# Causal attention and a routed feed-forward layer in one kernel: one set of transposes in place of two, and a table one slot later

## The chip, the cores and the metric

The kernel runs on one NeuronCore of a Trainium2 chip. The core has five engines that work side by side, each with its own queue in program order: TensorE (PE) multiplies matrices and transposes, VectorE (DVE) and ScalarE (ACT) work on elements and may read the accumulators in PSUM, GpSimd (POOL) works on elements in SBUF alone, and SyncE (SP) issues DMA transfers. An engine waits for another one by semaphores. The metric is the device time of one execution in microseconds (us), less is better.

## What is computed

The reference is causal attention for 8 batches, 12 heads, 448 tokens and 64 elements per head, followed by a layer of 8 experts in which each token goes to one expert and each expert keeps only its 80 tokens of largest weight:

```python
scores = np.where(mask, -1e9, scale * np.matmul(q, k.transpose(0, 1, 3, 2)))
attn = softmax(scores)
x = (attn @ v).transpose(0, 2, 1, 3).reshape(N, D)        # N = 3584 tokens, D = 768
logits = x @ w_gate                                        # 8 experts
expert_idx = np.argmax(logits, axis=1)
gate_w = probs[np.arange(N), expert_idx]
...
for e in range(E):
    tok_idx = np.where(expert_idx == e)[0]
    if len(tok_idx) > capacity:                            # capacity = 80
        gw = gate_w[tok_idx]
        tok_idx = tok_idx[np.argpartition(-gw, capacity)[:capacity]]
    out[tok_idx] = gate_w[tok_idx, None] * (np.maximum(x[tok_idx] @ w1[e], 0) @ w2[e])
```

The kernel must find, while attention still runs, the 80 best tokens of each expert. It does so batch by batch, with a table of the best 80 so far.

## The kernel before

**Attention in slots.** The 48 pairs of heads (8 batches of 6) run one after another, each in 8 slots. Slots 0 to 6 of a pair hold its seven blocks of scores (PE, L423 to L436, tile `sp`), each followed by a softmax on DVE (L445) and ACT (L448). In slots 0, 2, 4 and 6 PE also transposes a bank of the previous pair's weights (`tp`, L465, copied out by ACT, L477), and in slot 7 it multiplies weights and values of the pair before that (`xp`, L495). `sp` has three PSUM banks, `tp` two.

**Steps in slots.** Everything else is put into this run by a hand-written order. The dictionary `STEPS` gives for each step the slot, counted from the end of the batch that it belongs to, so 48 slots on is the same place for the next batch. The seventh batch has its own dictionary, `EARLY`, and the last one a written list, `TAIL`, which runs after attention. Within a slot the scores come first (in slot 6 of a pair, and so in slots 30 and 38 below, a turn of `tp` comes first, then the steps, then the scores), and steps of the earlier batch come before those of the later one. Each step's instructions stand in their engines' queues in just this order.

**The steps that matter here**, for one batch:

- `columns` (L698 to L708) writes on POOL the one-hot of each token's expert three times (`oh3`, L702) and the token's block and place (L703, L705) into `mv`.
- `parts` (L710 to L716) splits the token's gate weight on POOL into three bf16 parts in `mv`; its last instruction is L716.
- `r0t`, `r0c`: PE transposes `oh3` (four 128x128 bf16 transposes into a bank `selt`, L731) and DVE copies the 24 rows into `ex[:, 0]` (L734). `r1t`, `r1c` do the same for the three parts of the weight, into `ex[:, 1]`.
- `rl`, `lt` (L757 to L769): products of `ex[:, 0]` with the table's row, and DVE counts per token how many in the table are larger. `cp`, `ro` turn this into new places for the table.
- `c3w`, `c3l` to `c0w`, `c0l` (L742 to L750): all tokens of a batch against each other, four blocks, PE (tile `rn`) and then DVE. `gt` (L799) counts them.
- `rr`, `rr_more` (L846): DVE writes, in two halves, which token goes to which place. `tn` (L853): PE's products with these, which make the new table. `tab` copies it out (DVE, L873), `rp` transposes it (PE, L877), and `row` copies the row that the next batch's `rl` uses (DVE, L881). In the slots of the next batch, `tn`, `tab`, `rp` and `row` stand at 29, 30, 32 and 33.
- `rt` (L592) transposes finished attention rows, and DVE (L611) scales and stores them.

All PSUM tiles of these steps share two banks, `ps_m`. A tile gets the bank that was freed first in program order, that is, whose last reader comes first in it.

```python
nc.tensor.transpose(selt[:, t * P:(t + 1) * P], src, identb)               # L731
(nc.scalar.copy if last else nc.vector.tensor_copy)(bt.ex[0:3 * E, i], got[0][0:3 * E])   # L734
nc.tensor.matmul(rl[:, t, 0:sn], bt.ex[:, 0, t * P:(t + 1) * P], row[:, 0:sn], start=True, stop=True)   # L761
```

The splits of q and k for the next heads (L384 to L395, on DVE and POOL) run through the same queues; L387 is DVE's cast of k.

After attention the experts' two layers run (from L1127 on); the change does not touch them.

Of the kernel before, what the change touches and what calls it, by code (L numbers as in the profile page):

```python
# [10 lines left out]
BF16 = mybir.dt.bfloat16  # L11
# [6 lines left out]
P = 128  # L18
# [11 lines left out]
ROWGAP = 1  # L30
ROWS0 = [2, 3, 7, 13]
ROWS1 = [59, 62, 64, 65]
STEPS = {'gp': 18, 'gs': 18, 'lp': 21, 'lg': 22, 'logit': 23, 'shifted': 25, 'chosen': 26, 'sums': 27, 'one_hot': 28, 'weight': 28, 'weighted': 31, 'columns': 30, 'parts': 33, 'r0t': 32, 'r0c': 33, 'r1t': 34, 'r1c': 35, 'rl': 36, 'lt': 36, 'c3w': 38, 'c3l': 39, 'cp': 40, 'ro': 41, 'c2w': 41, 'c2l': 43, 'c1w': 43, 'c1l': 44, 'c0w': 46, 'c0l': 46, 'gt': 47, 'earlier': 51, 'own': 47, 'rank': 51, 'places': 63, 'places_more': 66, 'rr': 73, 'tn': 77, 'tab': 78, 'rp': 80, 'row': 81, 'rr_more': 75}
EARLY = {'gp': 18, 'gs': 18, 'lp': 21, 'lg': 21, 'logit': 22, 'shifted': 24, 'chosen': 26, 'sums': 27, 'one_hot': 28, 'weight': 29, 'weighted': 31, 'columns': 30, 'parts': 32, 'r0t': 33, 'r0c': 33, 'r1t': 34, 'r1c': 34, 'rl': 35, 'lt': 35, 'c3w': 36, 'c3l': 37, 'cp': 38, 'ro': 39, 'c2w': 39, 'c2l': 40, 'c1w': 40, 'c1l': 41, 'c0w': 41, 'c0l': 42, 'places': 43, 'places_more': 43, 'gt': 44, 'earlier': 44, 'own': 44, 'rank': 46, 'rr': 46, 'tn': 48, 'tab': 50, 'rp': 51, 'row': 52, 'rr_more': 46}
ROWS_EARLY = [22, 26, 29, 43]
THIRD = [0, 0, 2, 2, 4, 6, 8]
THIRD_NEXT = [0, 0, 6, 2, 6, 4, 8]
# [15 lines left out]
def attention_then_moe(  # L53
# [12 lines left out]
    nc = tc.nc  # L66
    B, _, NP, S = qT.shape
    N, D = out.shape
    E = wg.shape[2]
# [3 lines left out]
    NT = (S + P - 1) // P  # L73
# [24 lines left out]
    def bank(shape, dtype, name):  # L98
        return (ps_x or ps_m).tile(shape, dtype, name=name, tag="x" if ps_x else "misc")
# [20 lines left out]
    NV = 5  # L120
# [11 lines left out]
    for r in range(2):  # L132
        t = akeep.tile([P, OFF_L + NT * P], F32, name=f"prob{r}")
# [7 lines left out]
    for r in range(2):  # L141
        t = akeep.tile([P, NT, PH * P], F32, name=f"vt{r}")
# [61 lines left out]
    def piece_parts():  # L204

        got = []
        k = PIECES[len(wload)][3]
        got.append(piece())
        half = PW // k // 2

        def part(j, x):
            t, src = got[0]
            nc.sync.dma_start(t[:, j, x * half:(x + 1) * half], src[:, j, x * half:(x + 1) * half])
        return [lambda j=j, x=x: part(j, x) for j in range(k) for x in range(2)]


    mv = one_hots = mv_flat = oh_flat = expert_cols = tables = table_rows = None
    identb = before = dec = number = number_after = pnum = tbase = wgd = slots_e = slots_t = None
# [3 lines left out]
    lg = keep.tile([P, NT, H * E], F32, name="lg")  # L222
# [28 lines left out]
    def late_constants():  # L251


        def padded(shape, name):
            t = spool.tile(shape, BF16, name=name, tag=name, bufs=1)
            nc.gpsimd.memset(t, 0.0)
            return t

        def orders():
            nonlocal identb, before  # L260
            identb = const.tile([P, P], BF16, name="identb")
            nc.gpsimd.tensor_copy(identb, ident)

            before = const.tile([P, NT * P], BF16, name="before")
            nc.gpsimd.memset(before, 1.0)
            own = before[:, (NT - 1) * P:NT * P]
            nc.gpsimd.affine_select(own, own, [[-1, P]], ALU.is_gt, 0.0, base=0, channel_multiplier=1)

        def gate_weights():
            nonlocal wgd  # L270

            wgd = const.tile([P, NP, 4 * E], F32, name="wgd")
            nc.gpsimd.memset(wgd, 0.0)
            for i in range(2):
                for j in range(2):
                    nc.gpsimd.tensor_copy(wgd[j * DH:(j + 1) * DH, i:NP:2, 2 * i + j:4 * E:4],
                                          wg_sb[j * DH:(j + 1) * DH, i:NP:2, :])

        def slots():
            nonlocal mv_flat, mv, slots_e, slots_t  # L280
            many = max(1, NSL)
            slots_e = const.tile([SL, many, E, SL], COUNT, name="slots_e")
            slots_t = const.tile([P, many, NT, SL], COUNT, name="slots_t")
            for t, k in ((slots_e, E), (slots_t, NT)):
                nc.gpsimd.iota(t, [[SL, many], [0, k], [1, SL]], base=0, channel_multiplier=0,
                               allow_small_or_imprecise_dtypes=True)
            mv_flat = padded([P, (NT - 1) * NV * E + 2 * E + P], "mv")
            mv = mv_flat[:, 0:NT * NV * E].rearrange("k (t v e) -> k t v e", v=NV, e=E)

        def operands():  # L290
            nonlocal oh_flat, one_hots, expert_cols, tables, table_rows
            oh_flat = padded([P, (NT - 1) * 3 * E + P], "oh3")
            one_hots = oh_flat[:, 0:NT * 3 * E].rearrange("k (t v e) -> k t v e", v=3, e=E)
            expert_cols = padded([P, 2, NT * P], "ex")
            tables = [[padded([SL, 2 * E + P], f"tab{s}_{i}") for i in range(2)] for s in range(NSL)]
            table_rows = [[padded([P, SL], f"row{s}_{i}") for i in range(2)] for s in range(NSL)]

        return [orders, gate_weights, slots, operands]
# [392 lines left out]
    def select_groups(bt):  # L691

        b = bt.b
        last = b == B - 1
# [2 lines left out]

        def columns():  # L698
            oh = bt.oh
            m, oh3 = bt.m, bt.oh3 = mv, one_hots  # L700
            bc = [P, NT, E]
            eng.tensor_copy(oh3, oh.unsqueeze(2).to_broadcast([P, NT, 3, E]))  # L702
            nc.gpsimd.tensor_tensor(out=m[:, :, 0, :], in0=oh, in1=tbase[:, b, :].unsqueeze(2).to_broadcast(bc),  # L703
                                    op=ALU.mult)
            nc.gpsimd.tensor_tensor(out=m[:, :, 1, :], in0=oh, in1=pnum.unsqueeze(2).to_broadcast(bc), op=ALU.mult)  # L705
            bt.parts = sm("parts", [P, NT])
            bt.less = [sm(f"less{t}", [P, (t + 1) * P], BF16) for t in range(NT)]
            bt.ex = expert_cols  # L708
# [14 lines left out]
        def expert_rows(i):  # L723
            got = []

            def turn():
                selt = bank([P, NT * P], BF16, "selt")
                got.append(selt)
                for t in range(NT):
                    src = mv_flat[:, (t * NV + 2) * E:][:, 0:P] if i else oh_flat[:, t * 3 * E:][:, 0:P]  # L730
                    nc.tensor.transpose(selt[:, t * P:(t + 1) * P], src, identb)  # L731

            def copy():
                (nc.scalar.copy if last else nc.vector.tensor_copy)(bt.ex[0:3 * E, i], got[0][0:3 * E])  # L734
            return [turn, copy]


        def compare(t):
            w = (t + 1) * P
            got = []  # L740

            def weights():  # L742
                rn = bank([P, NT * P], F32, "rn")
                got.append(rn)
                nc.tensor.matmul(rn[:, 0:w], bt.ex[:, 0, t * P:w], bt.ex[:, 1, 0:w], start=True, stop=True)

            def less():
                nc.vector.scalar_tensor_tensor(
                    out=bt.less[t], in0=got[0][:, 0:w], scalar=bt.gw[:, t:t + 1],
                    in1=before[:, NT * P - w:NT * P], op0=ALU.is_lt, op1=ALU.mult, accum_out=bt.parts[:, t:t + 1])  # L750
            return [weights, less]
# [90 lines left out]
        def move(s):  # L842
# [43 lines left out]
            if not last and NSL == 1:  # L886
# [3 lines left out]

        run = lambda fs: lambda: [f() for f in fs]
        bt.lower, bt.moves = [], []
        r0, r1 = expert_rows(0), expert_rows(1)
        cmp = [compare(t) for t in reversed(range(NT))]
        tabs = [table_chunk(s) for s in range(NSL)] if b else []
        moves = [f for s in range(NSL) for f in move(s)]
        steps = {"columns": columns, "parts": parts, "r0t": r0[0], "r0c": r0[1], "r1t": r1[0], "r1c": r1[1],
                 "places": places, "places_more": places_more, "earlier": earlier, "own": own, "rank": rank}
        steps.update({"hold": hold, **{f"gt{t}": lambda t=t: later_part(t) for t in range(NT)}} if last else {"gt": later})
        for t in range(NT):  # L900
# [38 lines left out]
    for b in range(B):  # L939
        bt = Batch()  # L940
# [17 lines left out]
    def batch_plan(bt):  # L958
# [12 lines left out]
        if CAP:  # L971
            steps.update(select_groups(bt))
        for name, at in (EARLY if early else STEPS).items():
            if name in steps:
# [7 lines left out]
    with tc.manual_schedule():  # L982
# [25 lines left out]
        deferred, parts = [], []  # L1008
        for i, pr in enumerate(pairs):
            bt = pr.bt  # L1010
# [20 lines left out]
            for k in range(SLOTS):  # L1031
                behind = []
                if k < SLOTS - 1:
                    work, after = scores[k]
                    turn, copy, x = turns[TSLOT.index(k)] if turns and k in TSLOT else (None, None, "a")
# [20 lines left out]
                if i > 4 and k % 4 == 3:  # L1056
                    if not parts and len(wload) < WBUF:
                        parts = piece_parts()
# [14 lines left out]
        bt = batches[-1]  # L1073
        turns = transpose_groups(pairs[n - 1])
        before_last, last_one = values_group(pairs[n - 2]), values_group(pairs[n - 1])
        steps = dict(zip(("guard", "invert", "last_rows"), norms(bt, slice(0, NP))))
# [3 lines left out]
        if CAP:  # L1080
            steps.update(select_groups(bt))
# [27 lines left out]
        for i, x in enumerate(ROW_ENGINES):  # L1109
            g, t = divmod(i, NT)  # L1110
# [331 lines left out]
```

## Time and profile before

| | us |
|---|---|
| median of 3 runs | 466.85 (466.36 to 467.3) |
| the profiled execution | 466.07 |
| its span, first to last instruction | 464.2 |
| one batch in the repeating part, 184.30 to 224.75 | 40.45 |
| busy in this batch: PE, DVE, ACT, POOL | 39.99, 37.63, 35.38, 34.73 |

The profile is of one execution. A line of its timeline gives start, duration, engine, line of the kernel, operation, and output and inputs with their shapes; "x4" is four instructions merged, and brackets give the engine's idle time just before and what ended it. PE's matmuls (PE) and the loads of their stationary operand (PEld) have rows of their own. Durations of neighbours overlap a little, since an engine begins one instruction while the last drains.

### The profile page before, as it was taken

To read this page: it belongs to the slowest core of one execution; us is meant where nothing else is said; L and a number is where in the kernel's file an instruction comes from. 1 tells how busy PE (TensorE), PEld (TensorE's weight loads), DVE (VectorE), ACT (ScalarE), POOL (GpSimd) and SP (SyncE) were. 2 spreads that over 40 slices of the span, in tenths; PEclk is the share of its full clock that TensorE was granted. 3 is DMA by queue.
4 is the path that set the end of the run, shared out by engine and by line. 5 is a ranking of instruction groups with operands and counts; after the bars stand their busy time and mean duration, and the time that the engine had idled before them with its cause. 6 is when DMAs were issued, how large, how long until landed. Compare 5 with 4: busy or idle time off the path is not lost.

```text
span 464.2 us, 14187 instructions
## 1 busy us (share of the span) xinstructions
PE 441.8 (95%) x4981; PEld 346.8 (75%) x4981; DVE 413.1 (89%) x1285; ACT 392.4 (85%) x1077; POOL 310.3 (67%) x382
## 2 busy tenths in 40 slices
PE   4899999999999999999999999999989999999994
PEld 2566667866777786677777767777648999999994
DVE  6888899988998999899899989989579999999892
ACT  6898989878988997898889789888586989988792
POOL 7999999988987987898798789860145133410011
PEclk9999999999999999999999999999999999999999
DMA  7758899989769578966957997539937999999941
GB/s 221 185 153 238 249 262 299 280 248 306 202 207 305 161 232 259 265 182 213 297 165 225 264 260 200 178 129 373 413 130 254 399 390 395 394 422 423 424 163 44
DMA packets 42998, 120.84 MB, mean 260 GB/s; under 512 B 6146, under 2 KB 23810, under 8 KB 39472
## 3 DMA queue, kind: packets, MB, share of 16 engines
q1 hardware_dynamic: 41712, 116.21, 76.9%
q0 software_dynamic: 1056, 3.51, 2.4%
q8 instruction: 39, 0.64, 0.6%
q14 instruction: 31, 0.25, 0.2%
q10 hardware_dynamic: 160, 0.23, 0.2%
HBM read 96.36 MB, written 23.99 MB: 259 GB/s over the span
## 4 chain that ended last, share of the span: by engine, by line
PE 83%; DVE 6%; DMA 3%; ACT 3%; issue 2%; SPq 1%; POOLq 0%; DVEq 0%
PE xp L495 16%; PE tp L465 15%; PE sp L423 6%; PE sp L424 5%; PE rt L592 4%; PE op L1245 4%; PE op L1237 4%; PE hp L1237 3%; PE gp L545 3%; PE hp L1252 3%; PE hp L1251 3%; PE hp L1249 3%; PE sp L433 3%; DMA qk<-k_t 3%; DVE ns L445 2%
## 5 line engine op out<-in xcount | busy, mean ns | idle before, releaser
L448 ACT ACTIVATE prob<-ns,nb 128x128 f32<-128x128 f32 (+3 forms) x336 | 177.0, 529 | 22.6 <-DVE nb L445 20.1
L445 DVE CUSTOM_DVE_ANT_0 ns<-sp,mask 128x384 f32<-128x384 f32 (+2 forms) x288 | 116.0, 413 | 18.7 <-PE sp L424 14.7
L465 PE MATMUL tp<-ident,prob 128*128 128x128 f32 x768 | 118.1, 276 | 0.9 <-ACT prob L448 0.9
L477 ACT COPY PT<-tp 128x512 f32<-128x512 f32 x182 | 104.0, 572 | 17.5 <-PE sp L423 8.4
L395 POOL TENSOR_TENSOR qk<-qk,qk 128x448 f16<-128x448 f32 x92 | 97.3, 1080 | 13.1 <-DVE qk L387 7.4
L465 PEld LDWEIGHTS tp<-ident,prob 128*128 128x128 f32 x768 | 89.6, 142 | 11.4 <-ACT prob L448 1.9
L1165 DVE SCALAR_TENSOR_TENSOR wl<-wraw,wh 128x768 f16<-128x768 f32 (+1 forms) x91 | 92.0, 1067 | 2.5 <-ACT wh L1180 2.3
L495 PE MATMUL xp<-PT,vt 128*64 128x448 f32 (+3 forms) x768 | 91.2, 380 | 0.0
L495 PEld LDWEIGHTS xp<-PT,vt 128*64 128x64 f32 x768 | 53.8, 137 | 42.7 <-issue 22.6
L423 PE MATMUL sp<-qk 128*128 128x384 f16 (+2 forms) x288 | 75.8, 279 | 8.0 <-DVE qk L349 5.1
L1180 ACT ACTIVATE wh<-wraw 128x768 f16<-128x768 f32 (+1 forms) x91 | 78.9, 931 | 4.2 <-PE hp L1252 1.8
L424 PE MATMUL sp<-qk 128*128 128x384 f16 (+2 forms) x288 | 78.1, 277 | 1.6 <-DVE qk L349 0.8
L448 ACT ACTIVATION_READ_ACCUMULATOR prob<-ns,nb 128x1 f32 x336 | 63.9, 190 | 0.0
L1338 POOL DMA_INDIRECT out<-yo,idx x8 | 14.6, 1828 | 69.0 <-ACT yo L1335 65.1
L390 POOL TENSOR_TENSOR qk<-qk,qk 64x448 f16<-64x448 f32 x46 | 54.2, 1179 | 3.4
L391 POOL TENSOR_TENSOR qk<-qk,qk 64x448 f16<-64x448 f32 x46 | 51.0, 1108 | 3.2
L387 DVE CAST qk<-qk 128x896 f16<-128x896 f32 x46 | 41.2, 897 | 1.1 <-DMA qk<-k_t 1.1
L423 PEld LDWEIGHTS <-qk 128*128 128x128 f16 x288 | 28.5, 99 | 17.1 <-issue 8.6
L384 POOL CAST qk<-qk 64x896 f16<-64x896 f32 x40 | 37.4, 936 | 4.3 <-PE sp L436 3.1
L1249 PEld LDWEIGHTS <-wh 128*128 128x128 f16 x362 | 36.5, 101 | 0.0
L1251 PEld LDWEIGHTS <-wh 128*128 128x128 f16 x362 | 36.2, 100 | 0.0
L1252 PEld LDWEIGHTS <-wl 128*128 128x128 f16 x362 | 36.2, 100 | 0.0
(192 smaller groups left out, 926.8 us busy)
## 6 DMA issues: line engine op xcount, KB each, us to landing
wraw<-w SPq DMA_DIRECT2D x27, 1536.0 KB, 20.4
qk<-k_t SPq DMA_DIRECT2D x92, 224.0 KB, 5.9
out<-mask_l SPq DMA_DIRECT2D x56, 192.0 KB, 4.4
qk<-q_t SPq DMA_DIRECT2D x23, 448.0 KB, 4.4
vt<-v_t SPq DMA_DIRECT2D x24, 384.0 KB, 5.9
xs<-xr SPq DMA_DIRECT2D x42, 192.0 KB, 3.9
wraw<-w SPq DMA_DIRECT2D x24, 256.0 KB, 6.1
vt<-v_t SPq DMA_DIRECT2D x24, 64.0 KB, 5.5
```

The costliest lines, as they stand in the source:

```text
L390: nc.gpsimd.tensor_tensor(out=qa[hi, i], in0=qf[lo, i], in1=qa[lo, i], op=ALU.subtract)
L391: nc.gpsimd.tensor_tensor(out=qb[lo, i], in0=qf[hi, i], in1=qb[hi, i], op=ALU.subtract)
L395: nc.gpsimd.tensor_tensor(out=k_lo[j][:, i], in0=kf[j][:, i], in1=k_hi[j][:, i], op=ALU.subtract)
L423: nc.tensor.matmul(sp[:, 0:w], qx[:, p, t * P:w], kx[:, p, 0:w], start=True, stop=False)
L424: nc.tensor.matmul(sp[:, 0:w], qx[:, p, t * P:w], lx[:, p, 0:w], start=False, stop=True)
L445: pr.masked = nc.vector.tensor_tensor_reduce(out=ns[:, 0:w], in0=sp[:, 0:w], in1=m, scale=-1.0 / 8.0, scalar=HUGE, op0=ALU.add, op1=ALU.mi ...
L448: nc.scalar.activation(pr.P[:, off:off + w], ns[:, 0:w], AF.Exp, bias=nb, scale=-1.0, accum_out=total)
L465: nc.tensor.transpose(pr.tp[:, i], pr.P[:, off:off + P], ident)
L477: copy(dst, src)
L495: state["pe"] = nc.tensor.matmul(xp[rows, 0:w], st["vt"][:, c, p * P + j * DH:p * P + (j + 1) * DH], pr.PT[:, j, n0:n0 + w], start=(c == 0 ...
L1165: return nc.vector.scalar_tensor_tensor(out=l, in0=src, scalar=SW, in1=h, op0=ALU.mult, op1=ALU.subtract)
L1180: nc.scalar.activation(h, src, AF.Copy, scale=SW)
```

## The change

For the first seven batches `mv` now has 128 columns per block of tokens, in 16 groups of 8: groups 2 to 6 hold what `mv` held, groups 8 to 10 the one-hots, and the others stay zero. So four transposes of whole blocks bring both sets of rows at once: the one-hots to partitions 64 to 87 and the weight's parts to partitions 32 to 55 of one bank. DVE still makes two copies out of it, at slots 33 and 35 (seventh batch: 33 and 34). The step is called `r1t` and stands where `r0t` stood (slot 32, seventh batch 33), and `parts` moves ahead of it, from 33 to 31. `tn`, `tab`, `rp` and `row` each come one slot later (78, 79, 81, 82 of their own batch; 30, 31, 33, 34 of the next). In the seventh batch `c0w` and `c0l` move from 41 and 42 to 42 and 43. The last batch keeps its two sets.

```diff
-STEPS = {... 'parts': 33, 'r0t': 32, 'r0c': 33, 'r1t': 34, 'r1c': 35, ... 'tn': 77, 'tab': 78, 'rp': 80, 'row': 81, 'rr_more': 75}
-EARLY = {... 'parts': 32, 'r0t': 33, 'r0c': 33, 'r1t': 34, 'r1c': 34, ... 'c0w': 41, 'c0l': 42, ...}
+STEPS = {... 'parts': 31, 'r1t': 32, 'r0c': 33, 'rl': 36, 'lt': 36, 'r1c': 35, ... 'tn': 78, 'tab': 79, 'rp': 81, 'row': 82, 'rr_more': 75}
+EARLY = {... 'parts': 32, 'r1t': 33, 'r0c': 33, 'r1c': 34, ... 'c0w': 42, 'c0l': 43, ...}
...
-            mv_flat = padded([P, (NT - 1) * NV * E + 2 * E + P], "mv")
-            mv = mv_flat[:, 0:NT * NV * E].rearrange("k (t v e) -> k t v e", v=NV, e=E)
+            mv_flat = padded([P, NT * P + 4 * E], "mv")
+            mv = mv_flat[:, 0:NT * P].rearrange("k (t v e) -> k t v e", t=NT, e=E)
...
-            m, oh3 = bt.m, bt.oh3 = mv, one_hots
+            m = bt.m = mv[:, :, 2:2 + NV, :]
+            oh3 = bt.oh3 = one_hots if last else mv[:, :, 8:11, :]
...
-                    src = mv_flat[:, (t * NV + 2) * E:][:, 0:P] if i else oh_flat[:, t * 3 * E:][:, 0:P]
+                    src = mv_flat[:, t * P + 4 * E:][:, 0:P] if i else oh_flat[:, t * 3 * E:][:, 0:P]
...
-                (nc.scalar.copy if last else nc.vector.tensor_copy)(bt.ex[0:3 * E, i], got[0][0:3 * E])
+                nc.scalar.copy(bt.ex[0:3 * E, i], got[0][0:3 * E])
             return [turn, copy]
+
+        def both_rows():
+            got = []
+
+            def turn():
+                selt = bank([P, NT * P], BF16, "selt")
+                got.append(selt)
+                for t in range(NT):
+                    nc.tensor.transpose(selt[:, t * P:(t + 1) * P], mv_flat[:, t * P:(t + 1) * P], identb)
+
+            def copy(i):
+                r = 4 * E if i else 8 * E
+                nc.vector.tensor_copy(bt.ex[0:3 * E, i], got[0][r:r + 3 * E])
+            return [turn, lambda: copy(0), lambda: copy(1)]
...
-        r0, r1 = expert_rows(0), expert_rows(1)
+        rows = [f for i in range(2) for f in expert_rows(i)] if last else both_rows()
...
-        steps = {"columns": columns, "parts": parts, "r0t": r0[0], "r0c": r0[1], "r1t": r1[0], "r1c": r1[1],
+        steps = {"columns": columns, "parts": parts, **dict(zip(("r0t", "r0c", "r1t", "r1c") if last else ("r1t", "r0c", "r1c"), rows)),
```

More of the change, by code (lines that the diff above doesn't have):

```diff
@@ L32 @@
 ROWS1 = [59, 62, 64, 65]
-STEPS = {'gp': 18, 'gs': 18, 'lp': 21, 'lg': 22, 'logit': 23, 'shifted': 25, 'chosen': 26, 'sums': 27, 'one_hot': 28, 'weight': 28, 'weighted': 31, 'columns': 30, 'parts': 33, 'r0t': 32, 'r0c': 33, 'r1t': 34, 'r1c': 35, 'rl': 36, 'lt': 36, 'c3w': 38, 'c3l': 39, 'cp': 40, 'ro': 41, 'c2w': 41, 'c2l': 43, 'c1w': 43, 'c1l': 44, 'c0w': 46, 'c0l': 46, 'gt': 47, 'earlier': 51, 'own': 47, 'rank': 51, 'places': 63, 'places_more': 66, 'rr': 73, 'tn': 77, 'tab': 78, 'rp': 80, 'row': 81, 'rr_more': 75}
-EARLY = {'gp': 18, 'gs': 18, 'lp': 21, 'lg': 21, 'logit': 22, 'shifted': 24, 'chosen': 26, 'sums': 27, 'one_hot': 28, 'weight': 29, 'weighted': 31, 'columns': 30, 'parts': 32, 'r0t': 33, 'r0c': 33, 'r1t': 34, 'r1c': 34, 'rl': 35, 'lt': 35, 'c3w': 36, 'c3l': 37, 'cp': 38, 'ro': 39, 'c2w': 39, 'c2l': 40, 'c1w': 40, 'c1l': 41, 'c0w': 41, 'c0l': 42, 'places': 43, 'places_more': 43, 'gt': 44, 'earlier': 44, 'own': 44, 'rank': 46, 'rr': 46, 'tn': 48, 'tab': 50, 'rp': 51, 'row': 52, 'rr_more': 46}
+STEPS = {'gp': 18, 'gs': 18, 'lp': 21, 'lg': 22, 'logit': 23, 'shifted': 25, 'chosen': 26, 'sums': 27, 'one_hot': 28, 'weight': 28, 'weighted': 31, 'columns': 30, 'parts': 31, 'r1t': 32, 'r0c': 33, 'rl': 36, 'lt': 36, 'r1c': 35, 'c3w': 38, 'c3l': 39, 'cp': 40, 'ro': 41, 'c2w': 41, 'c2l': 43, 'c1w': 43, 'c1l': 44, 'c0w': 46, 'c0l': 46, 'gt': 47, 'earlier': 51, 'own': 47, 'rank': 51, 'places': 63, 'places_more': 66, 'rr': 73, 'tn': 78, 'tab': 79, 'rp': 81, 'row': 82, 'rr_more': 75}
+EARLY = {'gp': 18, 'gs': 18, 'lp': 21, 'lg': 21, 'logit': 22, 'shifted': 24, 'chosen': 26, 'sums': 27, 'one_hot': 28, 'weight': 29, 'weighted': 31, 'columns': 30, 'parts': 32, 'r1t': 33, 'r0c': 33, 'r1c': 34, 'rl': 35, 'lt': 35, 'c3w': 36, 'c3l': 37, 'cp': 38, 'ro': 39, 'c2w': 39, 'c2l': 40, 'c1w': 40, 'c1l': 41, 'c0w': 42, 'c0l': 43, 'places': 43, 'places_more': 43, 'gt': 44, 'earlier': 44, 'own': 44, 'rank': 46, 'rr': 46, 'tn': 48, 'tab': 50, 'rp': 51, 'row': 52, 'rr_more': 46}
 ROWS_EARLY = [22, 26, 29, 43]
```

## The prediction

> **What bounds the kernel now.** I read the page first: busy shares, then the chain that ended last, then the groups by line with shapes kept apart.
>
> ```profile
> PE 441.8 (95%) x4981; PEld 346.8 (75%) x4981; DVE 413.1 (89%) x1285; ACT 392.4 (85%) x1077; POOL 310.3 (67%) x382
> PE 83%; DVE 6%; DMA 3%; ACT 3%; issue 2%; SPq 1%; POOLq 0%; DVEq 0%
> ```
>
> TensorE (PE) carries 83% of the chain, but VectorE (DVE) is busy 89% of the time, so little room separates them. What counts is which of the two ends last in each of the few stretches that the change touches. The transposes and copies in question are these groups:
>
> ```profile
> L731 PE MATMUL selt<-identb,oh 128*128 128x128 bf16 x32 | 3.1, 219 | 1.1 <-DVE oh L702 1.1
> L731 PE MATMUL selt<-identb,mv 128*128 128x128 bf16 x32 | 3.1, 217 | 0.2
> L734 DVE COPY ex<-selt 24x512 bf16<-24x512 bf16 x14 | 5.7, 405 | 0.0
> ```
>
> Both sets of transposes exist for all eight batches; seven lose one. The 14 DVE copies all stay: **DVE gets no work taken off.**
>
> Batches 2 to 6 (of 1 to 8) repeat one pattern. I take the fourth, from 183.7 us on, and first its timeline on every engine around the two sets (columns: start, duration, what ran, and in brackets the idle time before it). I number slots from the batch's end, as the schedule does.
>
> ```profile
> 187.02 0.32 DVE L849 TENSOR_TENSOR rr<-rank,slots_t 128x160 bf16<-128x160 f16 x1
> 187.38 0.25 PE L862 MATMUL tn<-mv,rr 128*80 128x40 bf16 x2 [0.32 <-DVE rr L849]
> 188.52 0.24 POOL L703 TENSOR_TENSOR mv<-goh,tbase 128x32 bf16<-128x32 f32 x1
> 190.04 0.25 POOL L716 TENSOR_TENSOR mv<-grest,mv 128x32 bf16<-128x32 f32 x1
> 190.71 0.29 DVE L445 CUSTOM_DVE_ANT_0 ns<-sp,mask 128x128 f32<-128x128 f32 x1 [1.18 <-PE sp L424]
> 190.74 0.10 PEld L877 LDWEIGHTS <-tab 80*128 80x128 bf16 x1
> 191.53 0.29 DVE L445 CUSTOM_DVE_ANT_0 ns<-sp,mask 128x128 f32<-128x128 f32 x1
> 191.74 0.18 DVE L881 COPY row<-rp 24x80 bf16<-24x80 bf16 x1
> 191.85 0.40 DVE L734 COPY ex<-selt 24x512 bf16<-24x512 bf16 x1
> 192.04 0.24 PEld L731 LDWEIGHTS <-mv 128*128 128x128 bf16 x4 [0.24 <-issue]
> 192.18 0.60 DVE L387 CAST qk<-qk 128x896 f16<-128x896 f32 x1
> 192.24 0.10 PEld L423 LDWEIGHTS <-qk 128*128 128x128 f16 x1
> 192.72 0.41 DVE L445 CUSTOM_DVE_ANT_0 ns<-sp,mask 128x256 f32<-128x256 f32 x1
> 193.06 0.41 DVE L445 CUSTOM_DVE_ANT_0 ns<-sp,mask 128x256 f32<-128x256 f32 x1
> 193.16 0.28 PEld L761 LDWEIGHTS <-ex 128*128 128x128 bf16 x4
> 193.40 0.41 DVE L734 COPY ex<-selt 24x512 bf16<-24x512 bf16 x1
> ```
>
> The reader is to see three things. PE waits 0.32 for the second half of `rr` inside the table's products (`tn`). At 190.71 DVE has been idle for 1.18 and waits for PE, so whatever PE saves before that point moves DVE forward too. From there DVE runs without a gap through both copies, while PE's `rl` weights (193.16) need two things that DVE writes: `row` and the first copy.
>
> **Part by part: one slot later for `tn`, `tab`, `rp`, `row`.** `tn` goes from slot 29 to slot 30, where it stands behind four transposes of attention weights (0.42 of PE, the row of 199.83 below). Then PE reaches the second half of `rr` after its end at 187.34, and the 0.32 goes. What is late next: nothing before 190.71, where DVE's 1.18 of idle time says that all its earlier work is done. Gain there: 0.33 (bound above: 0.42, if the transposes fill the wait and its restart whole). POOL's `columns` must not overwrite `mv` before `tn` has read it; before, `tn` ended at 187.63, now 0.1 to 0.3 later, and `mv` is written from 188.52 on: 0.6 of cover.
>
> In the second batch the wait is longer:
>
> ```profile
> 106.13 0.31 DVE L849 TENSOR_TENSOR rr<-rank,slots_t 128x160 bf16<-128x160 f16 x1
> 106.50 0.25 PE L862 MATMUL tn<-mv,rr 128*80 128x40 bf16 x2 [0.64 <-DVE rr L849]
> ```
>
> `rr` ends at 106.44 whatever PE does, so only the 0.42 of the transposes put in front is won.
>
> **One set instead of two.** The second set costs PE 0.24 of gap (192.04) and 0.20 until the next load (192.24), 0.44 per batch. The set that stays now needs `parts`, that is POOL's L716. In the steady batch that ends at 190.29 and PE, 0.33 earlier, gets there at about 190.4: no wait worth counting.
>
> But `rl` behind it gets nothing of this 0.44. `row` used to be DVE's next piece after the comparison of slot 33 (191.74). Now it stands behind the first copy (0.33 start to start), the cast (0.54) and the softmax of slot 34 (0.34): 1.21 later, so it ends at 193.13 less 0.33. PE, 0.33 + 0.44 earlier, would load `rl`'s weights at 192.4 and now waits until 192.85 or more. `rl` takes the bank of `rp`, which program order frees before that of the set, so the second copy doesn't hold it.
>
> **The copies' partitions.** Before, both copies read partitions 0 to 23. Now they read 64 to 87 and 32 to 55. No row shows DVE reading PSUM anywhere but from partition 0. The nearest rows are an early pair of casts (L384) on the lower and the upper half of the partitions:
>
> ```profile
> 23.10 0.61 DVE L384 CAST qk<-qk 64x896 f16<-64x896 f32 x1
> 23.64 0.61 DVE L445 CUSTOM_DVE_ANT_0 ns<-sp,mask_l 128x448 f32<-128x448 f32 x1
> 24.18 0.07 DVE L445 DVE_READ_ACCUMULATOR2_ANT nb<- 128x1 f32 x1
> 24.28 0.81 DVE L384 CAST qk<-qk 64x896 f16<-64x896 f32 x1
> 25.13 0.29 DVE L445 CUSTOM_DVE_ANT_0 ns<-sp,mask 128x128 f32<-128x128 f32 x1
> ```
>
> The lower cast's successor starts 0.07 before the cast ends (23.71 against 23.64). The upper cast starts 0.03 after its predecessor's end, and its successor 0.04 after its own: 0.11 lost on each side, 0.22 per visit to other partitions. Bounds for a copy: nothing (it writes partition 0, and only its read has moved) and 0.22; below nothing is excluded, since the copy's work is the same. I take 0.22, the row's value, so 0.44 of DVE per batch, half of it ahead of `row`.
>
> [...]
>
> With 0.22 ahead of `row`, `rl` loads at 193.07 instead of 193.16, and PE leaves it about 0.1 ahead of before. DVE, however, is 0.44 − 0.33 = 0.11 late after the second copy, and there the path changes engine:
>
> ```profile
> 196.22 0.61 ACT L448 ACTIVATE prob<-ns,nb 128x384 f32<-128x384 f32 x1 [0.66 <-DVE nb L445]
> 199.21 0.57 ACT L477 COPY PT<-tp 128x512 f32<-128x512 f32 x1
> 199.83 0.42 PEld L465 LDWEIGHTS tp<-ident,prob 128*128 128x128 f32 x4 [0.29 <-ACT PT L477]
> ```
>
> ScalarE (ACT) waits 0.66 for DVE's softmax of slot 37, then works without a gap up to the copy ending at 199.78, and PE already waits 0.29 for that copy. So this wait ends last: what DVE is late, PE is late at 199.83. A steady batch ends 0.11 later than before (bounds: 0.42 earlier without the holds, 0.12 later). The second batch: 0.44 − 0.42, nothing.
>
> **The first batch** has no table, and POOL is behind:
>
> ```profile
> 69.66 0.32 PEld L731 LDWEIGHTS <-oh 128*128 128x128 bf16 x4
> 70.40 0.25 POOL L716 TENSOR_TENSOR mv<-grest,mv 128x32 bf16<-128x32 f32 x1
> 70.41 0.29 DVE L445 CUSTOM_DVE_ANT_0 ns<-sp,mask 128x128 f32<-128x128 f32 x1 [0.32 <-PE sp L424]
> 70.96 1.04 DVE L387 CAST qk<-qk 128x896 f16<-128x896 f32 x1
> 72.40 0.32 PE L423 MATMUL sp<-qk 128*128 128x384 f16 x1 [0.27 <-DVE nb L445]
> ```
>
> The one set must wait for POOL's end at 70.65 where the first set started at 69.66. The loads start 1.04 later and the next scores about 0.9, DVE waits for them (it already does, 0.32), and PE's scores at 72.40 wait for DVE (0.27), so the missing second set gives nothing back. With 0.22 of holds and a cast that may run up to 0.4 shorter than 1.04: 0.7 to 1.1 lost, I take 0.95.
>
> **The seventh batch.** Its wait is another one:
>
> ```profile
> 309.25 0.31 PEld L592 LDWEIGHTS rt<-ident,xu 128*128 128x128 f32 x3 [0.38 <-PE tn L862]
> 313.78 0.18 DVE L881 COPY row<-rp 24x80 bf16<-24x80 bf16 x1
> 314.44 0.28 PEld L761 LDWEIGHTS <-ex 128*128 128x128 bf16 x4
> 320.90 0.10 PEld L423 LDWEIGHTS <-qk 128*128 128x128 f16 x1 [1.03 <-issue]
> ```
>
> With `tn` behind them the `rt` transposes needn't wait; `tn` waits for that bank instead, 0.15 won. `row` moves behind the copy and one softmax (0.33 + 0.34 + 0.22), so `rl` loads 0.3 later than 314.44. The last comparison's product one slot later shortens the 1.03 before 320.90, but the count behind it (`gt`) needs a DVE comparison whose time doesn't move. I take +0.26 (bounds −0.15 and +0.4). The last batch's steps and copies stay as they are.
>
> **Sum:** 0.95 + 0 + 4 × 0.11 + 0.26 = 1.65 us later. The profiled execution took 466.07 (span 464.2 and 1.9 around it), so 467.7 on its base; the median of the three runs lies 0.78 above, so **468.5**.
>
> **The rivals.**
> - **A, the forecast:** 468.5, own range 467.3 to 469.4. Chance 0.54.
> - **B, reads of upper PSUM partitions hold nothing** (not slower). For it: those copies write partition 0, and every held row here also writes elsewhere. Then DVE is 0.33 early at slot 37, ACT and the transposes of 199.83 too: 0.75 − 0.42 − 4 × 0.36 − 0.15 = −1.3, 465.5. It decides from 0.33 of holds per batch downwards. Chance 0.28.
> - **C, `row` isn't late either,** and PE keeps both gains: −0.77 in each steady batch, −0.9, −0.5, and 0.75 in the first: 463.1. Against it: DVE has no gap between 190.71 and `row`. Chance 0.09.
> - **D, `rl` waits for the second copy,** should the set's bank be the one it gets: ready at 193.81 + 0.44 − 0.33, PE some 0.5 late in each of five batches, with the first and seventh 470.8. Against it: program order. Chance 0.09.
>
> That the change doesn't remove the transposes is excluded: seven batches call one helper with one set.
>
> **The numbers.** Leaving C and D out drops 0.18, so the range is A and B with their bounds: 464.8 to 469.6. A measurement of this kernel can tell about 0.2% (0.9 us) from no change. Slower by more: 0.41 of A, all of D, 0.50. Within: 0.12 of A, 0.08 of B, 0.20. Faster: 0.01 of A, the rest of B and C, 0.30.
>
> **What would show it.** The `tn` wait on `rr` gone in batches 3 to 6; `selt` matmuls 64 to 36; in the first batch a PE wait of about 1 us on POOL's L716; DVE copies that start 0.03 after their predecessor's end, not 0.08 before it, and so the softmax behind them; PE waiting for `row` (L881) before `rl`; the tp weights late in slot 46 waiting longer for ACT. If copies still overlap their neighbours, B holds. If L761 waits for L734's second copy, D. What would make it wrong altogether: a cast L387 that changes length beside POOL, since it lies in the same DVE stretch.

## The result and the profile after

The changed kernel is slower, and by three times what was forecast: 471.8 us (471.76 to 472.03, median of 4 runs) against 466.61 us (466.01 to 467.3), ratio 1.0102, 95% interval 1.0077 to 1.0126. The forecast was 468.5, its range ended at 469.6. The profiled execution has a span of 470.1 us where the kernel before had 464.2.

In the page of the kernel after, the busy shares, the chain that ended last and one group of VectorE (DVE) answer to the lines shown of before:

```profile
PE 442.7 (94%) x4953; PEld 345.4 (73%) x4953; DVE 418.3 (89%) x1285; ACT 391.7 (83%) x1077; POOL 307.9 (66%) x382
...
PE 76%; DVE 9%; issue 5%; DMA 4%; POOL 2%; ACT 2%; SPq 0%; POOLq 0%; DVEq 0%; ACTq 0%
...
L387 DVE CAST qk<-qk 128x896 f16<-128x896 f32 x46 | 45.0, 978 | 1.7 <-DMA qk<-k_t 1.7
```

The same group in the page of before:

```profile
L387 DVE CAST qk<-qk 128x896 f16<-128x896 f32 x46 | 41.2, 897 | 1.1 <-DMA qk<-k_t 1.1
```

The 28 transposes that went (4981 to 4953) left TensorE (PE) as busy as before, DVE has 5.2 us more to do with the same 1285 instructions, and of the chain's 83% of PE 7 points went to DVE, to POOL and to issue (time in which nothing shown was waited for). Of the 5.2 us, 3.8 lie in the casts L387, 46 instructions that the diff does not touch.

Where they lie shows in a table of stretches: from the MEMSET of `goh` in one batch (slot 28) to that in the next, with the busy time of the casts L387 alone. Columns: stretch, its length, casts, granted clock of PE (1.00 is full), DMA share, GB/s. Before:

```profile
67.02:107.27 40.25, 5.70 (x6) 1.00 0.96 285
107.27:147.71 40.44, 4.97 (x6) 1.00 0.84 245
...
188.16:228.60 40.44, 4.98 (x6) 1.00 0.79 233
...
309.95:338.09 28.14, 0.00 (x0) 1.00 0.94 368
```

After:

```profile
67.59:108.85 41.26, 4.45 (x6) 1.00 0.91 268
108.85:150.22 41.37, 6.09 (x6) 1.00 0.85 239
...
191.58:232.94 41.36, 6.09 (x6) 1.00 0.76 221
...
316.17:344.15 27.98, 0.00 (x0) 1.00 0.94 362
```

The first stretch is 1.0 longer, each of the next five 0.9, the seventh batch's 0.16 shorter. In the five, the casts take 1.1 longer, though their number and clock are the same. The first mark itself is 0.57 later (67.59 against 67.02), ahead of all steps that the change moves; over the fourteen profiles of this study it lies anywhere from 67.0 to 68.6, with two sets as with one, so this part is chance, and the accounts below are made in batches.

Two stretches of the fourth batch show what happens to the casts. First the timeline of before (start, duration), GpSimd's (POOL's) cast of slot 33 and both instructions of slot 49:

```profile
190.24 1.92 POOL L384 CAST qk<-qk 64x896 f16<-64x896 f32 x2
...
204.44 0.62 DVE L387 CAST qk<-qk 128x896 f16<-128x896 f32 x1
204.48 1.49 POOL L390 TENSOR_TENSOR qk<-qk,qk 64x448 f16<-64x448 f32 x1
```

and of after, with slots 32 to 36 ahead of it:

```profile
193.65 1.91 POOL L384 CAST qk<-qk 64x896 f16<-64x896 f32 x2
193.66 0.29 DVE L445 CUSTOM_DVE_ANT_0 ns<-sp,mask 128x128 f32<-128x128 f32 x1 [0.69 <-ACT PT L477]
194.65 0.08 DVE L445 DVE_READ_ACCUMULATOR2_ANT nb<- 128x1 f32 x1
194.76 0.42 DVE L749 COPY ex<-selt 24x512 bf16<-24x512 bf16 x1
195.11 0.93 DVE L387 CAST qk<-qk 128x896 f16<-128x896 f32 x1
196.07 0.42 DVE L445 CUSTOM_DVE_ANT_0 ns<-sp,mask 128x256 f32<-128x256 f32 x1
196.66 0.32 PE L776 MATMUL rl<-row,ex 128*128 128x80 bf16 x4 [0.70 <-DVE row L896]
197.00 1.82 POOL L391 TENSOR_TENSOR qk<-qk,qk 64x448 f16<-64x448 f32 x1
197.32 0.60 DVE L387 CAST qk<-qk 128x896 f16<-128x896 f32 x1
197.96 0.56 DVE L445 CUSTOM_DVE_ANT_0 ns<-sp,mask 128x384 f32<-128x384 f32 x1
...
208.05 1.04 POOL L390 TENSOR_TENSOR qk<-qk,qk 64x448 f16<-64x448 f32 x1
208.15 1.42 DVE L387 CAST qk<-qk 128x896 f16<-128x896 f32 x1
209.16 1.30 POOL L391 TENSOR_TENSOR qk<-qk,qk 64x448 f16<-64x448 f32 x1
```

In slot 49 the same two instructions meet in both kernels. Before, DVE's cast starts 0.04 first and takes 0.62, while POOL's L390 takes 1.49 instead of 1.04 (the median of its 46). After, L390 starts 0.10 first and keeps its 1.04; the cast takes 1.42, that is until 0.48 after L390's end. Of these two one pays in either kernel, not both. In slot 33 the cast now starts at 195.11, inside POOL's L384, which ends at 195.56, and again it ends 0.48 after that; before it started at 192.18, when L384 (190.24 to 192.16) had just ended, and took 0.60. The softmax at 193.66 and the copy at 194.76, which read PSUM, run inside L384 at the length that their like had before (0.29, and 0.42 against 0.40): only the cast is held up.

The order of the starts in the rows does not always tell who pays. At 197.00 POOL's L391 starts 0.32 ahead of the cast of 197.32, and still L391 pays (1.82 instead of 1.04) and the cast keeps its 0.60; in the kernel after, batches 2 to 6 all show it (L391 1.82 to 1.83, cast 0.60). This cast stands right behind a copy of `ex`; in e3, e4 and e10 below, too, an L390 or L391 that starts 0.06 to 0.21 ahead of a cast behind such a copy is the one that pays. What decides there stays open.

The chain says that this counts. In slot 49, the chain of before, from 201.8 to 210, has only PE rows; the chain of after has this:

```profile
207.95 0.28 DVE ns L445
208.23 0.01 DVE nb L445
208.24 0.51 DVE qk L387
208.74 0.17 issue
208.91 0.02 DVEq L611
208.93 0.56 issue
209.49 0.41 DVE ns L445
209.90 0.02 DVE nb L445
209.92 0.04 issue
209.97 0.32 PE sp L423
```

PE's scores at 209.97 wait for the softmax behind the long cast. The cast lasts from 208.15 to 209.57; the chain books 0.51 of it as DVE and most of the rest as issue.

### The profile page after: what moved, and what is told of

Read it like the earlier page. It is cut to its first block, busy times and chain, and to the rows that moved or that the text cites. A ratio compares the mean times of both kernels' runs of the same rounds, so it can differ in the third digit from the quotient of the medians.

```text
span 470.1 us, 14124 instructions
## 1 busy us (share of the span) xinstructions
PE 442.7 (94%) x4953; PEld 345.4 (73%) x4953; DVE 418.3 (89%) x1285; ACT 391.7 (83%) x1077; POOL 307.9 (66%) x382
## 4 chain that ended last, share of the span: by engine, by line
PE 76%; DVE 9%; issue 5%; DMA 4%; POOL 2%; ACT 2%; SPq 0%; POOLq 0%; DVEq 0%; ACTq 0%
PE xp L495 15%; PE tp L465 13%; PE sp L423 6%; PE sp L424 4%; DMA qk<-k_t 4%; PE op L1260 4%; PE rt L592 3%; PE op L1252 3%; PE hp L1252 3%; DVE ns L445 3%; PE gp L545 3%; PE hp L1267 3%; PE hp L1266 3%; PE hp L1264 3%; PE sp L433 3%
## 5 line engine op out<-in xcount | busy, mean ns | idle before, releaser
L465 PE MATMUL tp<-ident,prob 128*128 128x128 f32 x768 | 119.4, 277 | 1.7 <-ACT prob L448 1.3
L395 POOL TENSOR_TENSOR qk<-qk,qk 128x448 f16<-128x448 f32 x92 | 96.0, 1063 | 16.8 <-DVE qk L387 11.2
L391 POOL TENSOR_TENSOR qk<-qk,qk 64x448 f16<-64x448 f32 x46 | 54.5, 1185 | 3.2
L390 POOL TENSOR_TENSOR qk<-qk,qk 64x448 f16<-64x448 f32 x46 | 50.8, 1104 | 4.0 <-DVE qk L384 0.6
L387 DVE CAST qk<-qk 128x896 f16<-128x896 f32 x46 | 45.0, 978 | 1.7 <-DMA qk<-k_t 1.7
L384 POOL CAST qk<-qk 64x896 f16<-64x896 f32 x40 | 37.1, 928 | 7.8 <-PE sp L436 6.5
L423 PEld LDWEIGHTS <-qk 128*128 128x128 f16 x288 | 28.5, 99 | 15.8 <-issue 7.1
L424 PEld LDWEIGHTS <-qk 128*128 128x128 f16 x288 | 28.6, 99 | 12.8 <-issue 9.9
```

The lines of the kernel that those rows point to most:

```text
L390: nc.gpsimd.tensor_tensor(out=qa[hi, i], in0=qf[lo, i], in1=qa[lo, i], op=ALU.subtract)
L391: nc.gpsimd.tensor_tensor(out=qb[lo, i], in0=qf[hi, i], in1=qb[hi, i], op=ALU.subtract)
L395: nc.gpsimd.tensor_tensor(out=k_lo[j][:, i], in0=kf[j][:, i], in1=k_hi[j][:, i], op=ALU.subtract)
L423: nc.tensor.matmul(sp[:, 0:w], qx[:, p, t * P:w], kx[:, p, 0:w], start=True, stop=False)
L424: nc.tensor.matmul(sp[:, 0:w], qx[:, p, t * P:w], lx[:, p, 0:w], start=False, stop=True)
L465: nc.tensor.transpose(pr.tp[:, i], pr.P[:, off:off + P], ident)
```

## The experiments

**Theory P:** a cast L387 on DVE and an instruction on POOL exclude each other; the one that starts later waits for the whole of the other. The change shifts DVE against POOL by tenths of a microsecond: counted from the batch's mark, the cast of slot 49 starts at 16.57 instead of 16.28, L390 at 16.47 instead of 16.32. That turns the order round in slot 49; and in slot 33 the cast, which comes earlier, falls into L384. The theory is the author's reading of the rows above; what the two engines would share, no run shows. The rows of slots 49 and 33 agree with it, both ways round: behind the cast's 0.62 L390 takes 1.49, behind L390's 1.04 the cast takes 1.42, behind L384 0.93. The row of 197.00 agrees only if its start is not yet its turn, which no run here shows. **Theory R**, the rival, stays with the prediction's own steps: `row` is late and the copies are held, and the casts' length is slack.

All times are medians; each ratio is against runs of the kernel before on the same chip, where it took 466.61 (beside the kernel after), 466.97 (beside e1 to e4), 467.17 (e5 to e8) and 467.43 (e9 to e12). So times of different groups compare by their ratios or their batches. "Batch" is the stretch of the fourth batch as in the table above, "casts" the busy time of its six L387.

| run | us | ratio (95% interval) | batch | casts |
|---|---|---|---|---|
| before | 466.61 | 1 | 40.44 | 4.98 |
| after | 471.80 | 1.0102 (1.0077 to 1.0126) | 41.36 | 6.09 |
| e1 before, cast 0.2 later | 472.01 | 1.0100 (1.0069 to 1.0132) | 41.21 | 5.67 |
| e2 after, L390 earlier | 469.24 | 1.0048 (1.0034 to 1.0061) | 40.72 | 5.06 |
| e3 before, slots only | 466.18 | 0.9982 (0.9972 to 0.9992) | 40.38 | 5.44 |
| e4 after, old slots | 473.73 | 1.0140 (1.0117 to 1.0163) | 41.53 | 5.75 |
| e5 e2, first batch two sets | 468.04 | 1.0013 (1.0002 to 1.0024) | 40.76 | 5.07 |
| e6 e2, lower partitions | 468.37 | 1.0023 (1.0014 to 1.0033) | 40.64 | 5.19 |
| e7 e3, cast in slot 31 | 465.79 | 0.9970 (0.9956 to 0.9984) | 40.26 | 5.31 |
| e8 e2, cast in slot 31 | 467.33 | 1.0002 (0.9992 to 1.0013) | 40.36 | 4.84 |
| e9 e8 with e5 and e6 | 466.34 | 0.9977 (0.9966 to 0.9987) | 40.36 | 5.05 |
| e10 e4, L390 earlier | 470.32 | 1.0069 (1.0053 to 1.0084) | 40.91 | 4.73 |
| e11 e10, lower partitions | 469.08 | 1.0035 (1.0021 to 1.0048) | 40.69 | 4.73 |
| e12 e7, second cast earlier | 464.43 | 0.9941 (0.9928 to 0.9955) | 39.86 (third: 40.09) | 4.20 (third: 5.36) |

### e1 and e2: turning the order round, and back

```diff
 # e1, on the kernel before; used where h % HB == 1, which is slot 49
+def late_high():
+    for _ in range(2):
+        nc.vector.memset(state["late"], 0.0)
+    k_high(0)
```

> The kernel before with one thing added: two memsets of one element on VectorE ahead of the cast L387 of slot 49 (about 0.1 to 0.18 us of work per batch, from the 0.07 to 0.09 of the memset row L669). Theory P (a cast on VectorE and an instruction on GpSimd exclude each other, and the later of the two waits for the whole of the other): before, that cast starts 0.04 ahead of GpSimd's L390 (204.44 against 204.48), so 0.1 of lateness turns the order round; the cast goes from 0.62 to about 1.4, a steady batch gets 0.7 to 0.9 longer, the whole 4 to 5 us: 470.5 to 471.5. Theory R (the changed kernel's time comes from the late row and the held copies alone, a longer cast is slack): at most the memsets themselves, 0.18 x 6 = 1.1 us, 466.6 to 467.7.

```diff
 # e2, on the kernel after
-THIRD_NEXT = [0, 0, 6, 2, 6, 4, 8]
+THIRD_NEXT = [0, 0, 6, 1, 6, 4, 8]
```

> The kernel after, with GpSimd's first subtraction (L390, L391) of the third that begins in slot 49 put ahead of the two to three small rank instructions instead of behind them, so that GpSimd's L390 starts and ends some 0.8 us earlier. Theory P: the cast of slot 49 (1.42 in the kernel after) then finds GpSimd's L390 nearly done and takes 0.6 to 0.8; a steady batch goes from 41.37 to about 40.75, the whole from 471.8 to 468 to 469. Theory R: the batch stays at 41.37 and the time at 471.8.

The timeline of e1 in slot 49:

```profile
207.02 1.03 POOL L390 TENSOR_TENSOR qk<-qk,qk 64x448 f16<-64x448 f32 x1
207.03 0.20 DVE L399 MEMSET late<- 128x1 f32 x2
207.22 1.31 DVE L387 CAST qk<-qk 128x896 f16<-128x896 f32 x1
```

and of e2:

```profile
206.61 1.04 POOL L390 TENSOR_TENSOR qk<-qk,qk 64x448 f16<-64x448 f32 x1
207.55 0.62 DVE L387 CAST qk<-qk 128x896 f16<-128x896 f32 x1
207.73 1.34 POOL L391 TENSOR_TENSOR qk<-qk,qk 64x448 f16<-64x448 f32 x1
```

In e1 two memsets, 0.2 us a batch, turn the order round: the cast takes 0.69 longer, no other cast changes, and the batch is 0.77 longer, where theory P gave 0.7 to 0.9. The kernel became 5 us slower, half a microsecond above theory P's range and far beyond theory R's 1.1; five batches account for 3.8 of it, and where the rest arises was not followed up. In e2 the instructions of PE, ACT and DVE and their order are those of the kernel after, only POOL's order differs. The cast starts at the same place (16.58 after the mark), L390 0.83 earlier, and the cast is back at 0.62, the batch 0.64 shorter (41.36 to 40.72, forecast 40.75), and more than half of the 1.02% is gone. A later cast is shorter in e2, too (1.38 to 1.13), but it lies on the chain of neither. Theory R is out as the whole cause.

### e3 and e4: each half of the change alone

```diff
 # e3, on the kernel before
-'tn': 77, 'tab': 78, 'rp': 80, 'row': 81
+'tn': 78, 'tab': 79, 'rp': 81, 'row': 82
```

> The kernel before with only tn, tab, rp and row one slot later; two sets of transposes, copies from partition 0. The prediction's terms: 0.33 won in four batches, 0.42 in the second, 0.15 in the seventh, row still in time: 464.7. Theory P: VectorE reaches the cast of slot 33 some 0.4 earlier, where GpSimd's L384 still runs until 192.16, so that cast goes from 0.60 to about 1.0 and eats the gain; 466.0 to 467.0 while the cast of slot 49 stays at 0.62, and about 470 where that one turns too. Theory R (row late behind the copy and the cast): PE waits for row ahead of rl, and the time is 466.6 to 468.

e4 is the same edit the other way round, on the kernel after.

> The kernel after with tn, tab, rp and row back in the slots of before; one set, copies from partitions 64 and 32. Theory P: the 0.32 wait inside tn is back, row comes ahead of the first copy again, the cast of slot 33 falls behind GpSimd's L384 again and is back at 0.60; what decides is the cast of slot 49: 1.4 as in the kernel after gives 470 to 472, 0.6 gives 468 to 469. Theory R: with row early again PE no longer waits ahead of rl; only the held copies are left, 0.95 in the first batch and 0.44 in five others: 469.0 to 469.8 whatever the cast of slot 49 takes.

The timeline of e3 in slot 33:

```profile
190.69 1.91 POOL L384 CAST qk<-qk 64x896 f16<-64x896 f32 x2
192.01 1.07 DVE L387 CAST qk<-qk 128x896 f16<-128x896 f32 x1
```

e3 came out as theory P said: what the later `tn` wins, the cast of slot 33 takes (0.60 to 1.07), and 0.06 per batch is left of it. e4 lies above what either theory gave, 1.7 us over theory P's upper end. Theory P's number was put together wrongly there: the turned cast of slot 49 and the held copies add, and I had let one stand for both. e10 takes them apart.

### e10 and e11: the held copies by themselves

e10 is e4 with e2's edit, e11 is e10 with e6's.

> The kernel of e4 (473.73 us; one set, tn to row in the old slots) with GpSimd's first subtraction early as in e2. What is left against the kernel before are the held copies and the first batch. Theory P with the prediction's price of the copies (0.44 per batch, all of it on the path here, since the cast of slot 33 runs free at 0.60): 40.44 + 0.44 = 40.88 per batch, some 470.3 us. If the copies cost less on the path, or the set that is gone pays for them: 40.5 to 40.7, 468.5 to 469.5.

> The kernel of e10 with the columns' order of e6, so that the first copy reads from partition 0 and only the second is held. Here nothing behind the first copy can eat its 0.22: a batch 0.22 shorter than e10's, and the time 1.3 to 1.5 less. If the copies are not what costs, the same as e10.

The stretch of the fourth batch in e10:

```profile
190.58:231.49 40.91, 4.73 (x6) 1.00 0.79 233
```

The casts of slots 33 and 49 are as in the kernel before here (0.60 and 0.62; a later one is 0.25 shorter), and `row` is early. The batch is 0.47 longer than before's 40.44 where 0.44 was forecast, so nothing of the transposes that went shows in it. (e10 carries e2's edit, which was not run on the kernel before.) Taking one copy's holds away (e11) gives 0.22 back, as forecast; the time falls by 1.24, a little less than the 1.3 to 1.5 expected. From e10 to e4 the batch goes from 40.91 to 41.53, 0.62. Two casts are longer there, that of slot 49 (0.62 to 1.41) and a later one (1.14 to 1.37); only the first lies on the chain of e4.

### e5 and e6: the first batch, and the copies beside the cast of slot 33

```diff
 # e5, on e2
-rows = [f for i in range(2) for f in expert_rows(i)] if last else both_rows()
+rows = [f for i in range(2) for f in expert_rows(i)] if last or b == 0 else both_rows()
 # e6, on e2
-m = bt.m = mv[:, :, 2:2 + NV, :]
-oh3 = bt.oh3 = one_hots if last else mv[:, :, 8:11, :]
+m = bt.m = mv[:, :, 10:10 + NV, :]
+oh3 = bt.oh3 = one_hots if last else mv[:, :, 0:3, :]
...
-    r = 4 * E if i else 8 * E
+    r = 12 * E if i else 0
```

> The kernel of e2 (469.24 us) with two sets of transposes in the first batch alone, in the slots and from the partitions of before. If the first batch loses 0.95 us because its one set waits for GpSimd's L717, as the prediction has it, the time falls by 0.9 to 1.0 to 468.3, the first period from 41.43 to some 40.4, and the later batches stay at 40.73. If that wait only takes the place of another one, the time stays at 469.2.

> The kernel of e2 (469.24 us) with the columns of the one set ordered anew: the one-hots' copy reads partitions 0 to 23 instead of 64 to 87, the parts' copy 96 to 119 instead of 32 to 55. If only a change of partition group costs (0.11 on each side of a copy), the first copy and the instruction behind it are no longer held, 0.22 per batch; VectorE then comes 0.11 earlier to the cast of slot 33 and waits 0.11 longer there for GpSimd's L384, so that a batch goes from 40.73 to about 40.62 and the whole to about 468.5. If every copy out of the set costs the same, wherever it reads, nothing changes: 40.73 and 469.2.

e5's first stretch is 1.19 shorter than e2's (41.43 to 40.24) and the others are the same, so the wait and the holds of the first batch, which e5 takes back together, cost somewhat more than the forecast's 0.95. In e6 the batch fell by 0.08 where 0.11 was expected: the copy is no longer held, and the cast behind it waits 0.13 longer for L384 (casts 5.06 to 5.19). In e11, with nothing behind the copy to wait for, the same edit gave its 0.22.

### e7, e8, e9, e12: the casts out of POOL's way

```diff
 # e7 on e3, e8 on e2: first cast of the third in slot 31 instead of 33
+def cast_ahead(h, slot):
+    fs = ahead[h] = split_third(h)
+    later_on(slot, [fs[1]])
+    fs[1] = None
...
+if (i + 1) % PH == 0 and HB < g < NTH and g % HB == 0:
+    cast_ahead(g, (i + 1) * SLOTS - 1)
 # e12, on e7: the second cast in slot 34 instead of 35
+    later_on(slot + 3, [fs[2]])
```

> The kernel of e3 (466.18 us: two sets, tn to row one slot later) with the cast L387 of slot 33 moved to slot 31 in five batches, where VectorE waits for PE for about 0.7 us. Theory P (the 0.4 won at tn was eaten by that cast, which waited 0.47 for GpSimd's L384): 0.60 + 0.47 leave VectorE's busy stretch; PE keeps at least the 0.4, a batch goes from 40.38 to 39.6 to 40.0, the whole to 463.5 to 465; GpSimd's parts wait up to 0.5 for the cast, which the second set (1.7 later) doesn't feel. If the gain at tn was lost elsewhere (row late ahead of rl), the time stays at 466.2; if the cast of slot 49 turns, it rises by about 3.

> The kernel of e2 (469.24 us: one set) with the same cast in slot 31. Theory P: the 0.33 that this cast waited and its 0.60 leave VectorE's busy stretch, but GpSimd's parts now wait up to 0.5 for it, and the one set needs them at once: a batch goes from 40.73 to 40.2 to 40.6, the whole to 466.5 to 468.5. If the cast's length is slack: 40.73 and 469.2, or worse by the parts' lateness, 470 to 471.5.

> The kernel of e8 (467.33 us; one set, GpSimd's first subtraction early, the cast of slot 33 in slot 31) with the first batch's two sets of e5 and the columns' order of e6. If the costs stand side by side: 1.0 less in the first batch and, with the cast of slot 33 out of the way so that nothing eats it, 0.2 less in each of six batches: 465.0 (464.6 to 465.8), a batch at 40.15 to 40.2. If e8's batch is set by PE and ScalarE by now, only the first batch's 1.0 remains: 466.3.

> The kernel of e7 (465.79 us) with the second cast of that third one slot earlier (slot 34 instead of 35): in e7 it took 0.94 because GpSimd's L390 had started 0.58 ahead of it. Now it starts where GpSimd's L384 ends and ahead of L390: VectorE comes about 0.35 earlier to the softmax of slot 36, a batch goes from 40.25 to 39.9 to 40.15, the whole to 464 to 465.2. If PE and ScalarE set the batch by now: 465.8.

The timeline of e7 around slots 31 and 35:

```profile
189.16 0.61 DVE L387 CAST qk<-qk 128x896 f16<-128x896 f32 x1
189.22 0.66 POOL L714 TENSOR_TENSOR mv<-gow,mv 128x32 bf16<-128x32 f32 x1
...
192.34 1.03 POOL L390 TENSOR_TENSOR qk<-qk,qk 64x448 f16<-64x448 f32 x1
192.92 0.94 DVE L387 CAST qk<-qk 128x896 f16<-128x896 f32 x1
```

The stretches of the third and fourth batch in e12:

```profile
148.16:188.25 40.09, 5.36 (x6) 1.00 0.81 235
188.25:228.11 39.86, 4.20 (x6) 1.00 0.79 236
```

e7 missed: 0.12 per batch instead of 0.4 to 0.8. The first cast left, DVE came 0.46 earlier to the second (5.06 after the mark instead of 5.52), L390 came 0.41 later, and the two now met (0.60 to 0.94). Here POOL shows the same on one of its small instructions, too: L714, 0.25 elsewhere, takes 0.66 when a cast has started 0.06 ahead of it. e12 moves the second cast as well and gains most of what e7 had missed. It is the fastest version found, faster than both kernels: 0.9941 (0.9928 to 0.9955). Its batches alternate between 40.09 and 39.86, and with them their casts between 5.36 and 4.20. In the third batch the second cast waits for L384 (0.97); in the fourth it keeps its 0.60 and L384 pays, 2.77 for its two instructions instead of 1.91. Why the two take turns from batch to batch stays open. e8 fell inside its range and e9 fell short by 1.3 us: its batch is e8's 40.36 although the holds are fewer, and its casts went from 4.84 to 5.05, which is about the 0.2 that the freed copy gave. The other case of its expectation, that PE and ACT set e8's batch by now, named 466.3, and 466.34 came; the longer cast speaks for POOL instead, but no run separates the two.

## Why the prediction was wrong, point by point

A steady batch adds up from the runs: before 40.44; one set with its held copies +0.47 (e10, 40.91, which has e2's edit as well); `tn` to `row` one slot later −0.19 (e2, 40.72); the order in slot 49 turned +0.64 (after, 41.36). The forecast had +0.11.

- **The step that failed** is the steady batch's sum. It carried DVE's 0.11 of lateness from the second copy through ACT to the PE wait at 199.83 and stopped there, with every cast L387 at its old length on both sides. Two casts changed, by 0.33 (0.60 to 0.93) and 0.80 (0.62 to 1.42) in the rows above. The first ate most of what the later `tn` gave; the second, 16 slots behind the change, put 0.62 to 0.64 on each of five batches (e10 to e4, after to e2), more than any term of that sum. The prediction's closing sentence named the casts beside POOL as what would make it wrong altogether, and its fences held the row of 192.18; POOL's row beside it, which ended 0.02 earlier, is not among them, and no rival was made of it.
- **The wait of `tn` on `rr`:** right, it is gone in batches 3 to 6. The softmax of slot 32 starts 2.08 after the batch's mark (193.66 less 191.58) where it was 2.55 (190.71 less 188.16): 0.47 earlier, more than the forecast's 0.33 and its bound of 0.42.
- **The second set pays nothing back:** right. PE waits 0.70 for `row` ahead of `rl` (196.66), as the forecast had it and rival C had not. Even where `row` is early (e10), the batch isn't shorter for it.
- **The held copies:** right in kind and size, so rival B falls. The copy at 194.76 starts 0.03 after its predecessor's end (194.73), the softmax at 196.07 0.03 after the cast's end (196.04), the one at 197.96 0.04 after its predecessor's. Before, the first copy started 0.07 ahead of its predecessor's end (191.85 against 191.92), the softmax behind the cast 0.06 (192.72 against 192.78). So these two copies, which read PSUM from partitions 64 and 32, show the gaps of the upper cast of 24.28 (0.03 and 0.04), from which the forecast took its 0.22; on the path it is 0.47 per batch for both copies (e10), and 0.22 of it goes when the first reads from partition 0 (e10 to e11).
- **DVE's lateness is PE's:** right in mechanism up to where it was followed, but 0.28 instead of 0.11. ACT's softmax that waits for DVE and PE's weights behind it both come 0.28 later after the mark (weights 11.95, row below, instead of 11.67); the cast of slot 33 took 0.33 and `tn` gave 0.14 more than forecast. With slot 49's 0.64 that makes the 0.92 of the batch.

```profile
203.53 0.42 PEld L465 LDWEIGHTS tp<-ident,prob 128*128 128x128 f32 x4 [0.32 <-ACT PT L477]
```

- **The first batch:** right. The set waits for POOL's L717 (0.77 and 1.01 in the rows below, of the kernel after), and the stretch is 1.01 longer than before; 0.95 was forecast, bounds 0.7 to 1.1. Taken back on e2 (e5) it gives 1.19.

```profile
71.27 0.40 PE L745 MATMUL selt<-identb,mv 128*128 128x128 bf16 x4 [0.77 <-POOL mv L717]
71.27 0.23 PEld L745 LDWEIGHTS <-mv 128*128 128x128 bf16 x4 [1.01 <-POOL mv L717]
```

- **The seventh batch:** +0.26 forecast, 0.16 shorter in the table of stretches (28.14 to 27.98), at the lower bound of −0.15. The later slots alone make it 0.27 shorter (e3, 27.87), the rest of the change alone 0.14 longer (e10, 28.28), so the term of 0.3 for the late `row` is the doubtful one; no run took it apart.
- **Rival D:** `rl` waits for `row` (L896), not for the second copy. It falls, though its total lay nearest to the result. (Its terms add up to 470.6 rather than 470.8.)
- **The range:** its upper end, 469.6, does not come out of the terms. Their upper bounds (1.1, 4 × 0.12 and 0.4) add up to 2.0 us, that is 468.8.

Summed up, the five batches behind the first were to cost 0.44 and cost 4.6 (0.91 to 0.94 each); no other term of the change was off by more than 0.5.

## What to carry to other kernels

Where VectorE and GpSimd work side by side, look for pairs of rows that start within some tenths of each other and note who is first: such a pair can be a switch, and a small shift of either engine far ahead in the schedule can throw it for every batch: here 0.14 us of DVE against POOL, made 16 slots earlier. In this kernel the pairs were the casts from SBUF to SBUF (L387 takes 0.603 to 1.506 in the kernel after); softmaxes and copies that read PSUM kept their length beside POOL (there the 48 softmaxes of 128x448 take 0.604 to 0.625, the 14 copies of `ex` 0.415 to 0.420). Where the rows' starts lie close, read who pays from the durations and not from the order alone. So follow a shift of an engine through the whole period, not to the first place where another engine takes it over, and ask of each such pair whether its order still holds. And once a pair is found, move it apart on purpose: one slot for one GpSimd step was worth 0.6 us a batch here, and moving two casts, on the kernel before with the later slots, made the version that beats both kernels.

## What the runs showed that I had not expected

- A margin of 0.04 us (204.44 against 204.48) decided over 0.64 us in each of five batches, and 0.2 us of added work in a batch cost 0.77 (e1).
- Behind a long cast POOL's next instruction can be longer, too: in the kernel after, the cast of 208.15 ends at 209.57, 0.48 after L390 (209.09), and L391, which starts at 209.16, takes 1.30 against 1.04.
- Of the six casts per batch in the kernel before, two already take 1.38 and 1.14 where the others take 0.60 to 0.62. Both end 0.48 after an L391 of POOL that started ahead of them (at 208.23 and 217.50), just as slot 49's cast does in the kernel after, so by theory P they wait for POOL as well. In every second batch of e12 they take 1.12 and 0.62 with no edit of their own. What they cost the kernel is not shown, since no run moved them by themselves.
